# A windowed-attention and gated feed-forward kernel: queues ordered by a build-time list schedule, one load queue, f32 weight staging, filler matmuls

## The chip, the cores and the metric

One core of a Trainium2 chip runs the kernel. It has a matmul engine (TensorE, PE in the profile, with its weight loads shown as PEld), VectorE (DVE), ScalarE (ACT), GpSimd (POOL) and SyncE (SP), which issues DMAs. Each engine works through its own queue in order; semaphores order work between queues. The metric is the device time of one execution in microseconds, less is better.

## The reference

Four sequences of 768 tokens with 8 heads of 64 go through causal attention with a window of 128 keys and 4 "sink" keys that every query sees. The result, 3072 tokens of 512, goes through a feed-forward layer with a gated activation. All inputs and the output are f32.

```python
scores = scale * np.matmul(q, k.transpose(0, 1, 3, 2))
keep = is_sink | in_window            # pos < 4, or 0 <= query - key < 128
scores = np.where(keep, scores, -1e9)
a = softmax(scores)
x = np.matmul(a, v)                   # heads side by side: (3072, 512)
h = x @ w_in                          # (3072, 2048)
g = h * (1.0 / (1.0 + np.exp(-beta * h)))
out = g @ w_out                       # (3072, 512)
```

## The kernel before

The work is cut into 8 half-batches (hb) of 384 tokens; half-batch hb is half of sequence hb // 2. A half-batch of attention is 4 units u, each a pair of heads. The steps of the program, with their lines in the profile of before:

- **load** (L379) brings q, k and v in f32 into stage buffers, two of each. Half-batch 0 comes in small pieces (q and k by head pair, 192 KB each, v in three chunks of 256 KB), the others as whole q and k (768 KB) and three v chunks. **load_w** (L389) has GpSimd's DMA queue load the weights in 8 pieces of 1 MB and cast them to bf16 on the way.
- **cast** (L312 on DVE, L314 on ACT, L412 on POOL) makes bf16 copies: q and k to x16 (q_0, q_1, k_0, k_1 in the profile), v to vaug, which carries a column of ones.
- **T** (L432): 6 transposes of a unit on PE, then a copy to qkT. kS (L444) holds the sink keys, vS (L421) the sink values.
- **SC** (L485): the scores of a unit, 8 matmuls; exp on ACT into E (L495), two instructions; window masks on POOL (L501); a sink mask for the first half of a sequence (L509).
- **SS** (L519): scores against the sink keys, exp into ES (L522).
- **AV** (L547, L557): E and ES times v, with the sums from the column of ones; DVE takes the reciprocal (L561) and scales to onorm (L563).
- **OT** (L575): 3 transposes of onorm, then a copy to xT. When the four units of a half-batch are through, its 384 tokens are ready for the feed-forward part.
- **H** (HQ, L595): for a token block T_ (a half-batch) and one of 16 slices m of the hidden layer, 4 matmuls; tanh on ACT into t (L599), three buffers; the gate's product on DVE into g (L601). 64 H matmuls make a block.
- **O** (OQ, L613): 3 output tiles of a block, 16 matmuls each, in groups of 4; copy to osb, DMA out (L624).

A planner writes all queues while the program is built. It keeps an estimate of when each engine comes free (`G.free`) and asks in a loop which step's inputs and PSUM banks are ready; attention steps go before feed-forward steps, and H and O alternate. A step writes its matmuls and all that follows on the other engines at once, so each queue has the order in which steps were chosen. Where a copy can run on several engines, the one that would end first by the estimate is taken at that moment:

```python
def quickest(options):
    return min(options, key=lambda e: G.free[e] + options[e])
```

A cast of q, k or v is allowed on POOL only, but for half-batch 0, where DVE and ACT can take it. Loads are held back by bytes: `ordered` makes a load wait for the landing of an earlier one when more than `AHEAD_BYTES` = 3200000 lie between them, whichever queue that was on.

Of the kernel before, what the change touches and what calls it, by code (L numbers as in the profile page):

```python
# [22 lines left out]
class Op:  # L23
    __slots__ = ("eng", "fn", "deps", "signal", "count", "waits", "sem", "vc", "dma", "seq", "end")


class Graph:
# [3 lines left out]

    ENGINES = ("pe", "act", "dve", "gp", "sp")
    HOP = 180

    def __init__(self):
        self.ops = []
        self.writers = {}
        self.readers = {}
        self.last_x = {}
        self.n_dma = 0  # L40
        self.n_eng = {e: 0 for e in self.ENGINES}
        self.free = {e: 800.0 for e in self.ENGINES}
        self.dma_free = 0.0

    def add(self, eng, fn, ns=0, r=(), w=(), x=(), dma=None):

        o = Op()
        o.eng, o.fn, o.dma = eng, fn, dma
        o.signal, o.count, o.waits, o.vc = False, 0, [], None
        o.seq = self.n_eng[eng]  # L50
        self.n_eng[eng] += 1
        deps = []
        for k in r:
            ws = self.writers.get(k)
            assert ws, k
            deps += [(p, True) for p in ws.values()]
        for k in w:
            deps += [(p, False) for p in self.readers.get(k, {}).values()]
            deps += [(p, False) for p in self.writers.get(k, {}).values()]
        for k in x:  # L60
            deps += [(p, False) for p in self.last_x.get(k, {}).values()]
        o.deps = deps
        who = ("dma", self.n_dma) if dma else eng
        if dma:
            self.n_dma += 1
        for k in r:
            self.readers.setdefault(k, {})[who] = o
        for k in w:
            self.writers[k] = {who: o}
            self.readers[k] = {}  # L70
        for k in x:
            self.last_x.setdefault(k, {})[eng] = o
# [3 lines left out]
        if dma:  # L76
            self.free[eng] = at + (1150 if eng == "gp" else 550)
            self.dma_free = max(self.dma_free, at + 1100) + ns
            o.end = self.dma_free + 1000
        else:  # L80
            o.end = self.free[eng] = at + ns
        self.ops.append(o)
        return o

    def at(self, keys):

        t = 0.0
        for k in keys:
# [3 lines left out]
            t = max([t] + [p.end + self.HOP for p in ws.values()])  # L92
        return t

    def bank_at(self, k):
        return max([0.0] + [p.end + self.HOP for p in self.last_x.get(k, {}).values()])
# [83 lines left out]
def bass_streamingllm_window__then__act_swish_beta_kernel(  # L180
# [33 lines left out]
    _program(nc, G, sb, ps, q, k, v, moe_w_in, moe_w_out, moe_beta, out)  # L214
    G.resolve()
# [12 lines left out]
def _program(nc, G, sb, ps, q, k, v, w_in, w_out, beta, out):  # L228
    NU = 2 * NPAIR
    NSTG, NX, NV, NT, NE, NON, NG, NTT, NOS, NKS = 2, 2, 3, 8, 3, 3, 3, 3, 4, 4  # L230
# [24 lines left out]
    gt = sb("g", (128, NM, HALF), BF16, NG)  # L255
    tt = sb("t", (128, HALF), F32, NTT)
# [6 lines left out]
    AHEAD_BYTES = 3200000  # L263
# [22 lines left out]
    held = set()  # L286
# [18 lines left out]
    def quickest(options):  # L305

        return min(options, key=lambda e: G.free[e] + options[e])

    def copy_fn(eng, dst, src, scale=1.0):
        if eng == "dve":  # L310
# [3 lines left out]
        return lambda e: e.activation(dst, src, AF.Copy, bias=0.0, scale=scale)  # L314
# [29 lines left out]
    def beta_in():  # L344
        b_ = take(1)
# [6 lines left out]

    flight = []

    def ordered(nbytes):

        ahead, wait = 0, []
        for key, b_ in reversed(flight):
            ahead += b_
            if ahead > AHEAD_BYTES:  # L360
                wait = [key]
                break
        key = ("flight", len(flight))
        flight.append((key, nbytes))
        return wait, [key]

    def load(hb, n, i):
# [10 lines left out]
        wait, mine = ordered(dst.shape[0] * dst.shape[1] * dst.shape[2] * 4)  # L378
        add("act" if hb == 0 and n == "k" and i == 0 else "sp", lambda e: e.dma_start(dst, src), ns, r=wait,  # L379
# [418 lines left out]
```

## Time and profile before

| what | value |
|---|---|
| three runs | 249.97, 249.92 and 247.48 us, median 249.92 |
| profiled execution | 250.16 us |
| its span on the chip | 248.4 us |
| PE busy | 225.2 us, 91% |
| ACT, DVE, POOL busy | 164.4, 121.0 and 103.7 us |
| DMA | 29.69 MB counted, mean 120 GB/s; 27.27 MB read |

The profile shows one execution by instruction. A row of its timeline has the start and the length in us, the engine, the line of the kernel, the operation, output and inputs with shapes, and how many equal instructions the row merges; in brackets stand the engine's idle time ahead of it and what ended it. Matmuls overlap in the pipeline, so the length of one is more than the distance from one to the next.

### The profile page before, as it was taken

The page shows a single profiled execution, that of the slowest core. Times are in us where ns is not written, and L with a number is a line of the kernel's source. Part 1 is how long each engine was busy: PE and PEld are TensorE (multiplying, and loading weights), DVE is VectorE, ACT ScalarE, POOL GpSimd, SP SyncE. Part 2 cuts the span into 40 slices and gives each one's busy share as a digit, 9 for nine tenths or more (in the row PEclk, how much of TensorE's full clock was granted, in tenths as well). Part 3 has the DMA queues.
Part 4 walks back from the last instruction along what each step waited for, and adds up shares of the span by engine and source line. Part 5 has one row for each costly group of instructions (what it writes and reads, how often), then busy time and mean ns, then how long its engine had stood idle before and what let it go on. Part 6 is the DMA issues. An engine that isn't in the chain of part 4 may idle for free.

```text
span 248.4 us, 4941 instructions
## 1 busy us (share of the span) xinstructions
PE 225.2 (91%) x1862; PEld 131.7 (53%) x1889; DVE 121.0 (49%) x246; ACT 164.4 (66%) x296; POOL 103.7 (42%) x220
## 2 busy tenths in 40 slices
PE   2626898899998899999999999999999999999994
PEld 1415465565665567556575564655555555555531
DVE  2405375345567566467775465543533533453320
ACT  4754399827998688887976989754744644554420
POOL 7533391998773998718883423630000000000000
PEclk9999999999999999999999999999999999999999
DMA  6999899999999976700110101011111011111112
GB/s 199 219 215 296 180 181 249 239 256 264 303 244 267 314 189 210 163 3 4 45 45 0 45 0 45 0 45 42 42 42 45 1 44 45 42 42 42 45 44 84
DMA packets 49432, 29.69 MB, mean 120 GB/s; under 512 B 25840, under 2 KB 46336, under 8 KB 49408
## 3 DMA queue, kind: packets, MB, share of 16 engines
q1 hardware_dynamic: 44912, 24.98, 36.1%
q0 software_dynamic: 4224, 4.19, 10.5%
q8 instruction: 15, 0.25, 0.4%
q10 hardware_dynamic: 272, 0.20, 0.2%
q14 instruction: 9, 0.07, 0.1%
HBM read 27.27 MB, written 6.29 MB: 135 GB/s over the span
## 4 chain that ended last, share of the span: by engine, by line
PE 78%; ACT 7%; DMA 5%; DVE 3%; SPq 2%; issue 2%; POOL 1%; DVEq 0%
PE P L595 33%; PE P L613 30%; DMA v_stage<-in_v_dram 5%; PE P L557 4%; PE P L485 3%; ACT E L495 3%; PE P L432 3%; PE P L575 2%; SPq L379 2%; ACT qkT L314 1%; ACT t L599 1%; PE P L547 1%; DVE g L601 1%; DVE onorm L563 1%; PE P L519 1%
## 5 line engine op out<-in xcount | busy, mean ns | idle before, releaser
L601 DVE SCALAR_TENSOR_TENSOR g<-t,P 128x384 bf16<-128x384 f32 x128 | 69.8, 554 | 80.5 <-ACT t L599 67.0
L599 ACT ACTIVATE t<-P,hbeta 128x384 f32<-128x384 f32 x128 | 73.7, 588 | 43.7 <-PE P L595 39.3
L595 PE MATMUL P<-xT,w_in 128*128 128x384 bf16 x512 | 99.2, 332 | 0.6 <-DVE onorm L563 0.6
L613 PE MATMUL P<-w_out,g 128*128 128x512 bf16 x357 | 92.4, 379 | 2.7 <-ACT ES L522 0.7
L501 POOL TENSOR_SCALAR_AFFINE_SELECT E<-E 128x256 bf16<-128x256 bf16 (+1 forms) x112 | 52.3, 499 | 48.2 <-ACT E L495 47.8
L595 PEld LDWEIGHTS P<-xT,w_in 128*128 128x128 bf16 x512 | 49.5, 99 | 37.3 <-issue 2.2
L613 PEld LDWEIGHTS P<-w_out,g 128*128 128x128 bf16 x384 | 36.3, 98 | 35.6 <-DVE g L601 1.6
L495 ACT ACTIVATE E<-P 128x768 bf16<-128x768 f32 x64 | 45.2, 766 | 6.8 <-PE P L485 6.8
L557 PE MATMUL P<-vaug,E 128*128 128x65 bf16 x352 | 20.0, 199 | 6.7 <-DVE vaug L312 3.4
L557 PEld LDWEIGHTS P<-vaug,E 128*128 128x128 bf16 x352 | 17.5, 101 | 10.1 <-DVE vaug L312 3.6
L314 ACT ACTIVATE osb<-P 128x512 f32<-128x512 f32 x22 | 13.2, 598 | 13.5 <-PE P L613 13.2
L563 DVE TENSOR_TENSOR onorm<-P,rden 128x384 bf16<-128x384 f32 x32 | 17.8, 558 | 1.1
L314 ACT ACTIVATE qkT<-P 128x768 bf16<-128x768 bf16 x20 | 16.2, 828 | 1.4 <-PE P L432 1.4
L485 PE MATMUL P<-qkT 64*128 64x128 bf16 (+1 forms) x256 | 16.6, 251 | 0.1
L314 ACT ACTIVATE xT<-P 128x384 bf16<-128x384 bf16 x23 | 11.3, 497 | 6.8 <-PE P L575 6.7
L522 ACT ACTIVATE ES<-P 128x128 bf16<-128x128 f32 (+1 forms) x32 | 12.3, 402 | 3.9 <-PE P L519 3.7
L575 PE MATMUL P<-ident,onorm 128*128 128x128 bf16 x96 | 11.1, 230 | 2.5 <-DVE onorm L563 1.8
L412 POOL TENSOR_SCALAR_AFFINE_SELECT vaug<-v_stage 128x512 bf16<-128x512 f32 x21 | 13.3, 659 | 0.0
L485 PEld LDWEIGHTS P<-qkT 64*128 64x128 bf16 x256 | 8.9, 98 | 8.3 <-issue 3.6
L547 PE MATMUL P<-vS,ES 128*128 128x130 bf16 x64 | 13.0, 225 | 0.0
L312 DVE COPY qkT<-P 128x768 bf16<-128x768 bf16 x12 | 11.3, 952 | 1.8 <-PE P L432 1.6
L575 PEld LDWEIGHTS P<-ident,onorm 128*128 128x128 bf16 x96 | 7.4, 101 | 8.0 <-DVE onorm L563 2.5
(47 smaller groups left out, 124.5 us busy)
## 6 DMA issues: line engine op xcount, KB each, us to landing
v_stage<-in_v_dram SPq DMA_DIRECT2D x24, 256.0 KB, 6.2
out_dram<-osb SPq DMA_DIRECT2D x24, 256.0 KB, 2.0
q_stage<-in_q_dram SPq DMA_DIRECT2D x7, 768.0 KB, 6.2
k_stage<-in_k_dram SPq DMA_DIRECT2D x7, 768.0 KB, 8.3
w_in<-in_moe_w_in_dram POOLq DMA_DIRECT2D x4, 512.0 KB, 9.3
w_out<-in_moe_w_out_dram POOLq DMA_DIRECT2D x4, 512.0 KB, 7.3
q_stage<-in_q_dram SPq DMA_DIRECT2D x4, 192.0 KB, 3.7
k_stage<-in_k_dram SPq DMA_DIRECT2D x3, 192.0 KB, 4.3
```

The costliest lines, as they stand in the source:

```text
L314: return lambda e: e.activation(dst, src, AF.Copy, bias=0.0, scale=scale)
L485: add("pe", lambda e, dst=dst, kt=kt, kc=kc, rows=rows, q0=q0, nq=nq: e.matmul(dst, kt[rows, 1, kc:kc + 128], qkT[u % NT][rows, 0, q0:q0 + ...
L495: add("act", lambda e, src=src, dst_=dst_: e.activation(dst_, src, AF.Exp, bias=0.0, scale=SCALE), act_ns(256 * n), w=[(k_, z, j) for k_ i ...
L501: add("gp", lambda e, d=d, sg=sg, at_=at_: e.affine_select(d, d, [[0, 2 * len(at_)], [sg, 128]], ALU.is_ge, 0.0, base=min(sg, 0), channel_ ...
L547: add("pe", lambda e, m=m, c0=c0: e.matmul(A[:, c0:c0 + 2 * (D + 1)], ES[z][:, m * 128:(m + 1) * 128], vS[b % 2][:, 2 * hp:2 * hp + 2, :]. ...
L557: e.matmul(A[:, c0:c0 + D + 1], E[z][:, i, hh, :], vaug[vz][:, kb % NK, 2 * hp + hh, :], start=a, stop=o, skip_group_check=True), 39,
L563: add("dve", lambda e: e.tensor_tensor(onorm[on][:, :, :, :].rearrange("p m h d -> p (m h) d"), av[:, :, 0:D], rden[on][:, :].unsqueeze(2) ...
L575: add("pe", lambda e, m=m: nc.tensor.transpose(mp[:, m * 128:(m + 1) * 128], onorm[on][:, m, :, :].rearrange("p h d -> p (h d)"), ident[:, ...
L595: add("pe", lambda e, c=c: e.matmul(hp, w_in16[:, c, m * 128:(m + 1) * 128], xT[:, c, t0:t0 + HALF], start=(c == 0), stop=(c == 3)), mm_ns ...
L599: add("act", lambda e: e.activation(tt[ti][:, :], hp, AF.Tanh, bias=0.0, scale=hbeta[:, m:m + 1]), act_ns(HALF) + 93, r=["hbeta"], w=[("t" ...
L601: add("dve", lambda e: e.scalar_tensor_tensor(gt[T_ % NG][:, m, :], tt[ti][:, :], 1.0, hp, ALU.add, ALU.mult), dve_ns(HALF), r=[("t", ti)] ...
L613: add("pe", lambda e, m=m: e.matmul(P[:, bk, :], gt[T_ % NG][:, m, t * 128:(t + 1) * 128], w_out16[:, m, :], start=(m == 0), stop=(m == NM ...
```

## The change

The change keeps the steps and their arithmetic, and does six things.

1. **A list schedule.** The planner's loop still writes the program, but afterwards `Graph.arrange` orders every queue anew. PE's steps stay groups, of which the first three that are left can go next (`SKIP = 3`); an instruction of another engine can go as soon as its predecessors are planned; of those that can start first, the one with the longest tail behind it goes.
2. **Free engine choice.** A copy carries its alternatives (`alts`), and `arrange` takes the engine on which it would end first. Casts of q, k and v can now run on ACT, DVE or POOL; sink masks on POOL or DVE. The durations in these tables are new numbers.
3. **One load queue.** All loads are issued by SP, k's first piece too, which ACT issued before. `ordered` is gone. The order of loads is half-batches 0 and 1, then the weights.
4. **Weights in f32.** They come as 16 pieces of 512 KB by SP into six staging buffers (`wst`, three of them inside the g buffer of token block 2), and each is cast by ACT, DVE or POOL (`cast_w`). A piece's load waits for the cast of the piece six before it. H of block 2 is not written until all 16 are cast.
5. **The start is written out by hand**: the steps of half-batch 0 stand in a fixed order, with SC of unit 3 ahead of the AV steps. E has four buffers instead of three (`NE`).
6. **Filler matmuls**: 256-column matmuls of ones into PSUM bank 7, whose result nobody reads, stand where the plan has PE waiting, up to the last OT of half-batch 0. Bank 7 is held back for them until then.

```diff
+    def arrange(self):
...
+            for i, grp in enumerate(todo_pe[:self.SKIP]):
...
+                t, off = self.free["pe"], 0.0
+                for o in grp:
+                    t = max([t] + [p.end + self.HOP - off for p in o.preds if id(p) not in own and p.eng != "pe"])
+                    off += o.ns
+                if best is None or t < best[0] - self.SLACK:
+                    best = (t, "pe", i)
...
+            for o in pool:
+                opts = []
+                for e, (fn, ns) in o.alts.items():
+                    t = max(self.free[e], ready(o, e))
+                    if o.dma:
+                        t = max(t, self.dma_free - 3000)
+                    opts.append((t + ns, t, e))
+                _, t, e = min(opts)
+                by_eng.setdefault(e, []).append((t, o))
+            for e, c in by_eng.items():
+                t0 = min(c, key=lambda x: x[0])[0]
+                o = max((x for x in c if x[0] <= t0), key=lambda x: x[1].tail)[1]
+                if best is None or t0 < best[0]:
+                    best = (t0, e, o)
...
+                while self.filler and grp[0].group <= self.fill_to and self.free["pe"] + self.filler[0] <= t:
+                    o = self.filler[1]()
...
-    NSTG, NX, NV, NT, NE, NON, NG, NTT, NOS, NKS = 2, 2, 3, 8, 3, 3, 3, 3, 4, 4
+    NSTG, NX, NV, NT, NE, NON, NG, NTT, NOS, NKS, NWS = 2, 2, 3, 8, 4, 3, 3, 3, 4, 4, 6
...
+    wst = [w_[:, :, :] for w_ in sb("wst", (128, 2, 512), F32, NWS // 2)]
+    spare = gt[NG - 1][:, :, :].rearrange("p m t -> p (m t)").bitcast(F32).rearrange("p (z c f) -> p z c f", c=2, f=512)
+    wst += [spare[:, z, :, :] for z in range(NWS // 2)]
...
-    AHEAD_BYTES = 3200000
+    def any_of(alts, r=(), w=(), x=()):
+
+        return G.add(min(alts, key=lambda e: G.free[e] + alts[e][1]), None, 0, r, w, x, None, alts)
...
-    held = set()
+    held = {7}
...
-        add("act" if hb == 0 and n == "k" and i == 0 else "sp", lambda e: e.dma_start(dst, src), ns, r=wait,
-            w=[("stg", n, z, j) for j in keys] + mine, dma=f"d{n}{z}{'' if i is None else i}")
+        add("sp", lambda e: e.dma_start(dst, src), ns,
+            w=[("stg", n, z, j) for j in keys], dma=f"d{n}{z}{'' if i is None else i}")
...
-        add("gp", lambda e: e.dma_start(dst, src), 1048576 / 380, r=wait, w=[("w16", j)] + mine, dma=f"dw{j}")
+        add("sp", lambda e: e.dma_start(wst[j % NWS], src), 524288 / 370, w=[("wst", j % NWS)], dma=f"dw{j % NWS}")
+
+    def cast_w(j):
...
+        src_ = wst[j % NWS]
+        any_of(copies(dst, src_, {"act": 947, "dve": 602, "gp": 1060}), r=[("wst", j % NWS)], w=[("w16", m, h)])
...
+        if hb == 0 and n != "v":
+            ns = {"act": 413, "dve": 400}
         else:
-            fn = copy_fn(eng, dst, src)
-        add(eng, fn, opts[eng], r=r, w=w)
+            ns = {"act": 540, "dve": 340, "gp": 612}
+        any_of(copies(dst, src, ns), r=r, w=w)
...
-    LOADS = xl(0) + [0, 1, 2, 3] + xl(1) + [4, 5, 6, 7] + [x for hb in range(2, NSB) for x in xl(hb)]
+    LOADS = xl(0) + xl(1) + list(range(16)) + [x for hb in range(2, NSB) for x in xl(hb)]
...
+    G.fill(lambda e: e.matmul(P[:, 7, 0:256].rearrange("p (a b) -> p a b", a=2), ones[:, :],
+                              ones[:, :].unsqueeze(1).to_broadcast([128, 2, 128]), start=True, stop=True), ["ones"])
```

What this does to the queues is seen at three places. The first is SyncE's queue behind the small loads of half-batch 0; stage buffers ending in 1 belong to half-batch 1, and a name s_dw0 is the landing of weight piece 0. Before:

```order
L379 DMA v_stage0<-in_v_dram 128x8x64 x3
L379 DMA q_stage1<-in_q_dram 128x8x192 [waits s_dw0]
L379 DMA k_stage1<-in_k_dram 128x8x192 [waits s_dw1]
L379 DMA v_stage1<-in_v_dram 128x8x64 [waits s_dw2]
L379 DMA v_stage1<-in_v_dram 128x8x64 x2
L379 DMA q_stage0<-in_q_dram 128x8x192 [waits s_dw4]
```

And in the changed kernel, where wst and g2 are the weights' staging buffers:

```order
L491 DMA v_stage0<-in_v_dram 128x8x64 x3
L491 DMA q_stage1<-in_q_dram 128x8x192
L491 DMA k_stage1<-in_k_dram 128x8x192
L501 DMA wst0<-in_moe_w_in_dram 128x2x512
L501 DMA wst1<-in_moe_w_in_dram 128x2x512
L491 DMA v_stage1<-in_v_dram 128x8x64 x3
L501 DMA wst2<-in_moe_w_in_dram 128x2x512
L501 DMA g2<-in_moe_w_in_dram 128x2x512 x3
L501 DMA wst0<-in_moe_w_in_dram 128x2x512 [waits s_gp]
```

The loads of half-batch 1 no longer wait for weight landings; two weight pieces stand between its k and its v, and from the seventh piece on a load waits for a cast.

The second place is PE's queue from the last AV of half-batch 0 on. Before:

```order
L557 MATMUL P<-vaug,E 128x65 x6
L547 MATMUL P<-vS,ES 128x130
L557 MATMUL P<-vaug,E 128x65 x4
L575 MATMUL P<-ident,onorm 128x128 x3
L595 MATMUL P<-xT,w_in 128x384 x60
L432 MATMUL P<-ident,q_1 128x128 x3
```

In the changed kernel L671 and L661 are AV, L690 is OT, L885 the fillers, L548 T and L709 H:

```order
L690 MATMUL P<-ident,onorm 128x128 x3
L885 MATMUL P<-ones 128x256 x5
L690 MATMUL P<-ident,onorm 128x128 x3
L548 MATMUL P<-ident,q_1 128x128 x3
L548 MATMUL P<-ident,k_1 128x128 x3
...
L632 MATMUL P<-qkT,kS 128x384 x3
L600 MATMUL P<-qkT 128x2x128 x2
...
L709 MATMUL P<-xT,w_in 128x384 x8
L661 MATMUL P<-vS,ES 128x130
L671 MATMUL P<-vaug,E 128x65 x4
```

Half-batch 1's transposes and scores now stand ahead of the first H matmuls, and H comes in pieces between its AV steps; fillers stand only ahead of the last OT.

The third place is DVE's queue at half-batch 1 (L438 are casts and copies, L716 the product of H). Before, none of these casts was on DVE: behind onorm (L563) came 15 products (L601). Now:

```order
L438 CAST k_1<-k_stage 128x512
L438 COPY qkT<-P 128x768
L438 CAST w_in<-wst 128x2x512
L438 CAST vaug<-v_stage 128x8x64 x3
L675 RECIPROCAL rden<-P 128x6
L677 TENSOR_TENSOR onorm<-P,rden 128x384
L716 SCALAR_TENSOR_TENSOR g<-t,P 128x384 x2
L438 COPY xT<-P 128x384
L438 CAST w_in<-g 128x2x512
```

Casts of weights, of k and of v now stand in DVE's queue ahead of the products of H.

More of the change, by code (lines that the diff above doesn't have):

```diff
@@ L736, in _program @@
         now = G.free["pe"]
-        if not started and done["T"] >= 2:
-            beta_in()
-            started = True
         ffn = ("O", "H") if last == "H" else ("H", "O")
```

276 lines of the change are left out of this document (191 added, 85 removed).

## The prediction

> **What bounds the kernel now.** I read the profile from the coarse to the fine: its engine totals, a table of stages, then the timeline of TensorE around the first feed-forward matmul.
>
> ```profile
> PE 225.2 (91%) x1862; PEld 131.7 (53%) x1889; DVE 121.0 (49%) x246; ACT 164.4 (66%) x296; POOL 103.7 (42%) x220
> ...
> 0.00:26.00 26.00, 11.52 (x118) 8.10 (x119) 8.79 (x22) 13.46 (x25) 12.99 (x41) 1.00 1.04 232
> 26.00:54.40 28.40, 26.80 (x226) 15.43 (x227) 14.06 (x28) 19.56 (x33) 19.84 (x36) 1.00 1.00 215
> 54.40:172.90 118.50, 115.35 (x1151) 71.16 (x1166) 69.27 (x144) 95.73 (x177) 70.89 (x145) 1.00 0.45 121
> 172.90:248.40 75.50, 71.50 (x374) 36.99 (x379) 28.94 (x52) 35.66 (x61) 0.00 (x0) 1.00 0.11 43
> ```
>
> After the stage's length stand the busy times of PE, PEld, DVE, ACT and POOL, then granted clock, DMA share and GB/s. From 54.4 to 172.9 PE idles 118.50 - 115.35 = 3.15 us in all. The matmuls are the bound there, and there is little left to take. The first 26 us are another regime: PE is busy 11.52 of 26.00, while the DMA engines are full (share 1.04). So the start is limited by data. Its chain:
>
> ```profile
> 4.82 0.95 POOL L389 DMA_DIRECT2D w_in<-in_moe_w_in_dram  x1
> 4.84 4.10 SPq L379 DMA_DIRECT2D v_stage<-in_v_dram  x3
> ...
> 15.06 0.63 ACT L314 ACTIVATE vaug<-v_stage 128x512 bf16<-128x512 f32 x1 [1.37 <-DMA v_stage<-in_v_dram]
> 19.19 0.43 DVE L312 CAST vaug<-v_stage 128x512 bf16<-128x512 f32 x1 [5.01 <-DMA v_stage<-in_v_dram]
> 19.67 0.68 PE L557 MATMUL P<-vaug,E 128*128 128x65 bf16 x9 [3.42 <-DVE vaug L312]
> 25.51 0.50 PE L575 MATMUL P<-ident,onorm 128*128 128x128 bf16 x3 [0.88 <-DVE onorm L563]
> 25.81 12.34 PE L595 MATMUL P<-xT,w_in 128*128 128x384 bf16 x60
> ...
> 172.91 3.41 PE L595 MATMUL P<-xT,w_in 128*128 128x384 bf16 x20
> 176.16 1.03 PE L613 MATMUL P<-w_out,g 128*128 128x512 bf16 x4
> ```
>
> The third v chunk of half-batch 0, issued behind 4.84, lands only at 19.19, because the weight loads of GpSimd's queue share the DMA engines from 4.82 on. AV of unit 0 waits for it 3.42 us, OT of unit 3 runs at 25.51, and H starts at 25.81. Its first 60 matmuls take 12.34 us. At 172.91 twenty take 176.16 - 172.91 = 3.25 us, 0.1625 each, so 60 would be 9.75. The missing 2.6 us are matmuls at half rate, which the clock column does not show (1.00 everywhere); the durations do.
>
> **The change, part by part.** I compare both kernels at one milestone: half-batches 0 and 1 through OT and the 64 H matmuls of token block 0. Before, it lies behind OT of unit 7, and 32 O matmuls are done by then (groups of 4, 4, 4, 4, 8, 8; some records are missing):
>
> ```profile
> 42.00 0.81 PE L613 MATMUL P<-w_out,g 128*128 128x512 bf16 x3 [0.74 <-ACT ES L522]
> ...
> 52.52 1.89 PE L613 MATMUL P<-w_out,g 128*128 128x512 bf16 x7
> 54.25 0.33 PE L575 MATMUL P<-ident,onorm 128*128 128x128 bf16 x3
> 54.41 1.03 PE L613 MATMUL P<-w_out,g 128*128 128x512 bf16 x4
> ...
> 237.98 7.30 PE L613 MATMUL P<-w_out,g 128*128 128x512 bf16 x33 [0.26 <-DVE g L601]
> ```
>
> One O matmul is (7.30 - 0.38)/32 = 0.216 us (the last one's own 0.38 taken off), 32 are 6.9. Before, the milestone without O is therefore at 54.4 - 6.9 = 47.5 us. For the changed kernel I walk there:
>
> ```profile
> 8.15 1.30 ACT L495 ACTIVATE E<-P 128x768 bf16<-128x768 f32 x2 [0.65 <-PE P L485]
> 9.03 1.31 POOL L501 TENSOR_SCALAR_AFFINE_SELECT E<-E 128x256 bf16<-128x256 bf16 x3 [1.25 <-ACT E L495]
> 9.33 0.53 ACT L314 ACTIVATE q_0<-q_stage 128x384 bf16<-128x384 f32 x1
> 9.74 0.28 ACT L522 ACTIVATE ES<-P 128x128 bf16<-128x128 f32 x1
> ...
> 20.06 0.20 DVE L561 RECIPROCAL rden<-P 128x6 f32<-128x6 f32 x1
> 20.29 0.56 DVE L563 TENSOR_TENSOR onorm<-P,rden 128x384 bf16<-128x384 f32 x1
> ...
> q1 hardware_dynamic: 44912, 24.98, 36.1%
> q0 software_dynamic: 4224, 4.19, 10.5%
> ...
> 60.00:80.00 20.00, 19.21 (x197) 12.03 (x199) 11.74 (x26) 17.94 (x35) 13.02 (x25) 1.00 1.05 262
> ...
> q1 hardware_dynamic: 1439, 2.62, 10.0%
> ```
>
> *Half-batch 0.* No weights are in front any more: 2.36 MB of q, k and v from about 2 us on, at the 262 GB/s of the saturated stage 60 to 80, end at 11.0, so the last v chunk lands near 12. It is no longer last. What is last is ScalarE: four units of 1.30 + 0.28 and one cast of 0.53 are 6.85 us in one queue; from 8.6 (8.15, plus half a microsecond since k's first load now stands behind q's on SyncE) to 15.5. GpSimd's three selects of unit 3 end about 1 us later, 16.3; then AV 0.5, reciprocal and norm 0.76 and two handovers: OT of unit 3 at 17.9 instead of 25.5.
>
> *Half-batch 1.* A k cast stands on ScalarE behind the four xT copies, so the 24 transposes T start near 19.1. Three of the four qkT copies queue on ScalarE, 1.50/2 = 0.75 us each in the first row below: from the first unit's transposes at 19.5 to 22.0. SC of the second unit (0.44) and the first 8 H matmuls (1.3) follow, to 23.9.
>
> ```profile
> 38.66 1.50 ACT L314 ACTIVATE qkT<-P 128x768 bf16<-128x768 bf16 x2
> 40.23 0.50 PE L485 MATMUL P<-qkT 64*128 64x256 bf16 x8
> 40.67 0.59 PE L519 MATMUL P<-qkT,kS 128*128 128x384 bf16 x2
> 44.32 0.22 PE L547 MATMUL P<-vS,ES 128*128 128x130 bf16 x1
> 44.85 0.33 PE L519 MATMUL P<-qkT,kS 128*128 128x384 bf16 x1
> ...
> L412 POOL TENSOR_SCALAR_AFFINE_SELECT q_1<-q_stage 128x512 bf16<-128x512 f32 x12 | 7.5, 659 | 0.0
> L312 DVE CAST vaug<-v_stage 128x512 bf16<-128x512 f32 x1 | 0.4, 429 | 5.0 <-DMA v_stage<-in_v_dram 5.0
> ```
>
> The first AV of this half-batch also needs v1, behind 5.77 MB of one queue: 2 + 22.0 + 1 = 25.0 at 262 GB/s, somewhat earlier since 1 MB of it is weights. I take 24.5. From there the work in the written order is AV 4 x 0.53 (44.85 - 44.32), SC 2 x 0.44 (40.67 - 40.23), OT 4 x 0.16 (54.41 - 54.25) and 56 H matmuls, 9.1: 12.8 us. One weight piece is cast on GpSimd between two units' selects; a 1024-element cast has no row, twice the 0.66 above is its upper end and once the lower; with the selects ahead of it I add 1.2. Milestone: 38.5. That is 24.5 + 12.8 + 1.2. Against 47.5 the **gain is 9.0 us**.
>
> *Weights.* The 16 pieces of 512 KB are the unknown, as no f32 weight load stands in the trace. The nearest row is 2 KB packets out of SBUF (170 to 240 us): 2.62 MB in 10.0% of 70 us, 374 GB/s, 1.40 us a piece. The old weight queue read 8.39 MB in 10.5% of 248.4 us: 1.63 a piece. The slow end is the mixed 262 GB/s, 2.0 a piece. I take 1.5, near the first two: the last piece, 14 behind v1, lands at about 45 and is cast by DVE at 45.7. O of block 0 wants it at 38.5 + three O groups 2.6 + 32 H matmuls 5.2 = 46.3. Just hidden. At 2.0 it is 24.5 + 28 + 0.7 = 53.2, and of the 9.0 us only 2.1 are left. Each load waits for the cast six pieces earlier; six times 1.5 leaves 9 us for a slot to be landed, cast and issued again. Behind a waiting weight load SyncE holds all loads of half-batch 2: at 1.5 its q and k land 6 us after the last weight, 51, and its T stands 12.8 us of matmuls behind the milestone, at 51.3. So this too is just hidden, and slips by what the weights slip.
>
> *Fillers.* 47 matmuls of 256 columns, about 0.11 us each at full rate by the O matmul, 0.22 at half. All stand before OT of unit 3, where ScalarE's chain is late, not PE; cost nothing. Without that cover they would cost 5 to 10 us. If they keep PE at full rate, the 2.6 us of slow H are gone; this is inside the walk, which uses full-rate prices from 19 us on. Bank 7, held for them, leaves seven; SC takes four. The fourth E buffer lets SC of unit 3 go ahead of AV, which is in the walk.
>
> *Casts moved.* GpSimd loses 44 of its 63 casts at 0.66 (29 us), and DVE takes most, at 0.43, and seven more qkT copies. DVE's 58% of the stage 54 to 173 (69.27 of 118.50) becomes about 75%, ScalarE stays at 81%. Both stay below PE. The wider choice and the lookahead over three groups can save up to the 3.15 us of PE idle; a queue order fixed from planned times can as well add as much. I take no change, and keep -3 and +3.
>
> *The end.* From 172.9 on the order is H and O alone in both. No change.
>
> **Sum.** The profiled execution took 250.16 us, 1.7 beyond its span of 248.4. 250.16 - 9.0 = 241.2; the median of the runs is 0.24 lower than the profiled one, so **241.0**.
>
> **Rivals.**
>
> *Weights pace PE* (0.14). The mixed rate holds, or a cast stands late in its queue and holds its slot: up to 250.16 - 2.1 - 0.24 = 247.8. For it: before, SyncE also stood idle for handovers, below. Against: the 374 GB/s.
>
> ```profile
> SPq L379 <- DMA w_in<-in_moe_w_in_dram: 13.0, 3, 5.6
> SPq L379 <- DMA w_out<-in_moe_w_out_dram: 12.1, 3, 7.1
> SPq L379 <- POOL vaug L412: 9.4, 3, 6.5
> ...
> v_stage<-in_v_dram SPq DMA_DIRECT2D x24, 256.0 KB, 6.2
> ```
>
> *The slow rate comes back* (0.14). Between OT of unit 3 and AV of unit 4 PE has pauses and no fillers; before, a PE busy less than half of 26 us ran at half rate, and needed 5 us of unbroken H to leave it (2.6 us lost at half rate). Then T, SC and H until 24.5 take up to 4 us more, of which the wait for v1 hides most, and another 4.6 us at half rate cost 2.3: together about 3.6, 244.6. Against: PE idled 1.6 us of 26.0 to 54.4 (28.40 - 26.80), in pieces, and H kept its 0.16 spacing at 172.91. [...]
>
> *Slower: casts that wait in DVE's queue* (0.09). The order is fixed, and DVE now holds most q, k and v casts between the g products of H. One cast whose load is late stops every g behind it; three t buffers cover about 2 us, then PE stops. v chunks land 6.2 us (median, the row above) after their issue, so a late issue costs up to 4.2. In each of half-batches 2 to 7 an average of 1.5 us decides: 6 x 1.5 = 9.0. At 2.1 it is 253.6. Against: a half-batch is loaded in 9 us and used in about 20, and SyncE runs ahead.
>
> *It doesn't do what it says* (0.07): the planned start is not reached, since the planner's durations are shorter than the measured ones (413 ns for the k cast that took 0.53 us), and the lists hold each other up: 249.9.
>
> **How the numbers follow.** Forecast 0.50 (239 to 243.5); a middle stage without its idle time, 238, 0.06; the rivals as above. The range goes from 236.5, the forecast with idle and a start 1.5 us better, to 248.5, the slow weights: it leaves out the slower case and a part of the last. About 1% is what a measurement of this kernel can tell from no change, so faster means below 247.4: the forecast, the better middle stage, the clock case and most of the weights case, 0.80; same 0.11; slower 0.09.
>
> **What would show it.** First H matmul near 22 us with 0.16 us spacing; OT of unit 3 near 18; the last v chunk of half-batch 0 cast by 14; OT of unit 7 near 38.5; the last weight cast by 46; PE idle of about 3 us from there to the last attention unit. The prediction is wrong if H is spaced 0.32 us, if PE waits for weight casts beyond 40 us, or if g waits for DVE's casts in the middle.

## The result, and the profile after

| kernel | median of its runs (range) | profiled execution | span |
|---|---|---|---|
| before | 248.70 us (246.9 to 249.97, 4 runs) | 250.16 us | 248.4 us |
| after | 240.71 us (240.04 to 240.98, 4 runs) | 240.98 us | 239.3 us |

The ratio is 0.968, with a 95% interval of 0.9601 to 0.9759. Measured again later beside other kernels, after took 240.43 us (6 runs). The forecast was 241.0. The total came out as forecast, but the terms of the sum did not: the start won 2.8 us less than forecast, and 2.9 us came from two stretches that the sum had put at nothing.

The engine totals of after, then its table of stages in the columns used above: the start up to 26 us, to the milestone (OT of unit 7), to the last attention unit, and the rest. After's figures stand in the order span, PE, PEld, DVE, ACT, POOL, clock, DMA share, GB/s.

```profile
PE 228.4 (95%) x1936; PEld 132.3 (55%) x1936; DVE 149.4 (62%) x305; ACT 163.7 (68%) x293; POOL 79.6 (33%) x172
...
q1 hardware_dynamic: 49536, 33.57, 48.6%
```

```profile
0.00:26.00 26.00, 20.93 (x235) 13.68 (x236) 16.42 (x35) 17.58 (x33) 16.97 (x47) 1.00 0.96 252
26.00:42.10 16.10, 13.84 (x133) 8.17 (x130) 13.78 (x30) 13.23 (x24) 7.78 (x14) 1.00 1.03 374
42.10:160.00 117.90, 117.51 (x1169) 70.94 (x1168) 88.65 (x186) 94.27 (x171) 54.88 (x113) 1.00 0.57 151
160.00:239.30 79.30, 76.12 (x410) 39.49 (x405) 30.59 (x56) 38.63 (x67) 0.00 (x0) 1.00 0.12 44
```

In the middle PE now idles 117.90 - 117.51 = 0.39 us, where it idled 3.15 before. From 26.0 to 42.1 it still idles 16.10 - 13.84 = 2.26 us, and DVE is the fullest engine beside it, 13.78 of 16.10. All traffic but instructions runs in one queue, and the weights come at 374 GB/s. PE's busy time rose by 3.2 us although the slow H are gone, since the fillers are in it (47 records, 8.8 us together).

The timeline of after around the milestone, PE and then DVE and ACT:

```profile
18.08 0.34 PE L690 MATMUL P<-ident,onorm 128*128 128x128 bf16 x3 [0.63 <-DVE onorm L677]
...
23.92 1.47 PE L709 MATMUL P<-xT,w_in 128*128 128x384 bf16 x8
25.23 0.22 PE L661 MATMUL P<-vS,ES 128*128 128x130 bf16 x1
...
30.04 2.45 PE L709 MATMUL P<-xT,w_in 128*128 128x384 bf16 x14 [0.80 <-DVE w_in L438]
...
33.70 1.80 PE L709 MATMUL P<-xT,w_in 128*128 128x384 bf16 x10 [0.19 <-DVE w_in L438]
...
41.96 0.34 PE L690 MATMUL P<-ident,onorm 128*128 128x128 bf16 x3 [1.10 <-DVE onorm L677]
```

```profile
13.20 0.62 DVE L438 CAST vaug<-v_stage 128x512 bf16<-128x512 f32 x1
...
24.21 0.70 DVE L438 CAST vaug<-v_stage 128x512 bf16<-128x512 f32 x1 [0.43 <-DMA v_stage<-in_v_dram]
...
29.11 0.87 DVE L438 CAST w_in<-g 128x1024 bf16<-128x1024 f32 x1 [0.90 <-DMA g<-in_moe_w_in_dram]
...
40.68 0.19 DVE L675 RECIPROCAL rden<-P 128x6 f32<-128x6 f32 x1
40.79 0.65 DVE L438 CAST w_out<-g 128x1024 bf16<-128x1024 f32 x1
41.35 0.55 DVE L677 TENSOR_TENSOR onorm<-P,rden 128x384 bf16<-128x384 f32 x1
...
46.55 1.05 ACT L433 ACTIVATE w_out<-wst 128x1024 bf16<-128x1024 f32 x1
```

The third v chunk of half-batch 0 is cast at 13.20 instead of 19.19, OT of unit 3 stands at 18.08 instead of 25.51, the first H at 23.92. Eight H take 1.31 us (23.92 to 25.23), 0.164 each, full rate. Then PE waits twice for casts of w_in; ahead of the first of these, at 29.11, DVE itself stands idle 0.90 us until the piece of w_in has landed. The last OT waits for onorm, which stands in DVE's queue behind a cast of w_out. At the end, nothing waits between the last H and the last 36 O matmuls:

```profile
226.89 1.46 PE L709 MATMUL P<-xT,w_in 128*128 128x384 bf16 x8
228.19 7.93 PE L729 MATMUL P<-w_out,g 128*128 128x512 bf16 x36
```

Before had two pauses there, one ahead of the row at 237.98 and one ahead of this:

```profile
237.33 0.39 PE L613 MATMUL P<-w_out,g 128*128 128x512 bf16 x1 [0.25 <-DVE g L601]
```

To compare kernels whose matmuls stand in different orders I keep a **ledger**: the time at which a step starts on PE, less the time that all matmuls ahead of it in PE's queue need at their full-rate distance (H 0.1625 us, O 0.216, attention's by their rows, fillers nothing). What is left, an estimate, is what PE lost until then. Differences between columns give the loss of a stage.

| profiled execution | OT of unit 3 at | lost there | lost at OT of unit 7 | lost at OT of unit 31 | lost at PE's end |
|---|---|---|---|---|---|
| before | 25.51 | 20.03 | 24.79 | 29.25 | 30.17 |
| after | 18.08 | 12.60 | 18.54 | 20.95 | 21.01 |
| after, again | 17.98 | 12.50 | 17.51 | 19.81 | 19.87 |

So 24.79 - 18.54 = 6.25 us were won up to OT of unit 7, 4.46 - 2.41 = 2.05 in the middle and 0.92 - 0.06 = 0.86 in the last stretch; together 9.16, the fall of PE's end from 245.28 to 236.12. The start of one and the same kernel scatters by about 1 us between executions.

### The profile page after: what moved, and what is told of

Read it like the earlier page. It is cut to its first block, busy times and chain, and to the rows that moved or that the text cites. A ratio compares the mean times of both kernels' runs of the same rounds, so it can differ in the third digit from the quotient of the medians.

```text
span 239.3 us, 4895 instructions
## 1 busy us (share of the span) xinstructions
PE 228.4 (95%) x1936; PEld 132.3 (55%) x1936; DVE 149.4 (62%) x305; ACT 163.7 (68%) x293; POOL 79.6 (33%) x172
## 4 chain that ended last, share of the span: by engine, by line
PE 80%; SPq 9%; DVE 4%; DMA 3%; ACT 2%; issue 1%
PE P L729 34%; PE P L709 31%; SPq L491 7%; PE P L600 4%; PE P L548 4%; PE P L671 3%; DMA g<-in_moe_w_in_dram 3%; PE P L690 2%; SPq L501 2%; DVE g L716 1%; PE P L632 1%; PE P L661 1%; ACT t L714 1%; ACT E L609 1%; DVE w_in L438 1%
## 5 line engine op out<-in xcount | busy, mean ns | idle before, releaser
L716 DVE SCALAR_TENSOR_TENSOR g<-t,P 128x384 bf16<-128x384 f32 x128 | 69.9, 552 | 59.2 <-ACT t L714 56.6
L709 PE MATMUL P<-xT,w_in 128*128 128x384 bf16 x512 | 98.5, 326 | 1.1 <-DVE w_in L438 1.0
L729 PE MATMUL P<-w_out,g 128*128 128x512 bf16 x384 | 97.3, 379 | 0.0
L615 POOL TENSOR_SCALAR_AFFINE_SELECT E<-E 128x512 bf16<-128x512 bf16 (+1 forms) x112 | 54.5, 516 | 56.1 <-ACT E L609 55.3
L709 PEld LDWEIGHTS P<-xT,w_in 128*128 128x128 bf16 x512 | 48.0, 98 | 37.5 <-DVE w_in L438 1.8
L609 ACT ACTIVATE E<-P 128x768 bf16<-128x768 f32 x64 | 45.7, 769 | 3.1 <-PE P L600 2.8
L438 DVE COPY qkT<-P 128x768 bf16<-128x768 bf16 x19 | 18.0, 951 | 4.0 <-PE P L548 4.0
L671 PE MATMUL P<-vaug,E 128*128 128x65 bf16 x352 | 18.8, 193 | 0.8 <-DVE vaug L438 0.7
L433 ACT ACTIVATE osb<-P 128x512 f32<-128x512 f32 x21 | 12.5, 597 | 10.2 <-PE P L729 10.1
L671 PEld LDWEIGHTS P<-vaug,E 128*128 128x128 bf16 x352 | 16.7, 97 | 3.4 <-DVE vaug L438 0.9
L433 ACT ACTIVATE xT<-P 128x384 bf16<-128x384 bf16 x20 | 9.9, 495 | 6.7 <-PE P L690 6.7
L600 PEld LDWEIGHTS P<-qkT 64*128 64x128 bf16 x256 | 8.6, 94 | 10.6 <-issue 5.1
L433 ACT ACTIVATE qkT<-P 128x768 bf16<-128x768 bf16 x13 | 10.2, 814 | 5.2 <-PE P L548 5.1
L690 PE MATMUL P<-ident,onorm 128*128 128x128 bf16 x96 | 10.7, 220 | 2.3 <-DVE onorm L677 2.2
L661 PE MATMUL P<-vS,ES 128*128 128x130 bf16 x64 | 12.7, 220 | 0.0
L690 PEld LDWEIGHTS P<-ident,onorm 128*128 128x128 bf16 x96 | 7.0, 98 | 7.7 <-DVE onorm L677 4.2
L885 PE MATMUL P<-ones 128*128 128x256 bf16 x47 | 8.8, 323 | 1.1 <-POOL ones L444 1.1
```

What stands on the lines that cost most here:

```text
L438: return lambda e: e.tensor_copy(dst, src)
L600: add("pe", lambda e, dst=dst, kt=kt, kc=kc, rows=rows, q0=q0, nq=nq: e.matmul(dst, kt[rows, 1, kc:kc + 128], qkT[u % NT][rows, 0, q0:q0 + ...
L609: add("act", lambda e, src=src, dst_=dst_: e.activation(dst_, src, AF.Exp, bias=0.0, scale=SCALE), act_ns(256 * n), w=[(k_, z, j) for k_ i ...
L615: add("gp", lambda e, d=d, sg=sg, at_=at_: e.affine_select(d, d, [[0, 2 * len(at_)], [sg, 128]], ALU.is_ge, 0.0, base=min(sg, 0), channel_ ...
L671: e.matmul(A[:, c0:c0 + D + 1], E[z][:, i, hh, :], vaug[vz][:, kb % NK, 2 * hp + hh, :], start=a, stop=o, skip_group_check=True), 39,
L690: add("pe", lambda e, m=m: nc.tensor.transpose(mp[:, m * 128:(m + 1) * 128], onorm[on][:, m, :, :].rearrange("p h d -> p (h d)"), ident[:, ...
```

## The experiments

**Theory A:** the start was won by the order of loads and of the lists together; the middle and the end by the lookahead over three PE groups. Rivals: the fillers' clock, the spread of casts over engines, the f32 staging.

### Fillers, arrangement, lookahead, casts: after with one part taken away

`nofill`: no filler matmuls.

```diff
-    G.fill(lambda e: e.matmul(P[:, 7, 0:256].rearrange(...), ones[:, :], ...
```

> The changed kernel without its 47 filler matmuls, nothing else. Theory A (the fillers keep the matmuls at full rate from 6 us on): without them PE is busy too little until the first unbroken H, so transposes, scores and H between 19 and about 30 us run at half rate; 56 matmuls of H and half-batch 1 then cost 2.5 to 4 us more: 243.5 to 245, H spaced 0.32 us at first. Rival (the start is paced by loads and casts, PE's rate is hidden in the waits): 240.5 to 241.5 even with H spaced 0.32 us.

Measured: 240.60 us (240.09 to 240.97), ratio 0.9671 [0.9605, 0.9737]; the same as after. Theory A's price for the fillers falls. The matmuls do run slower without them. Three transposes of half-batch 0, first in after, then here:

```profile
9.63 0.33 PE L548 MATMUL P<-ident,q_0 128*128 128x128 bf16 x3
```

```profile
9.64 0.50 PE L548 MATMUL P<-ident,q 128*128 128x128 bf16 x3
```

The clock column reads 1.00 in both, as it does in the first 26 us of before. At 16.70 three take 0.33 us here too, and then the granted clock falls. Stages of this kernel around T of half-batch 1, columns as above:

```profile
16.80:20.00 3.20, 1.54 (x23) 1.06 (x20) 1.78 (x5) 1.75 (x4) 1.63 (x2) 1.00 1.13 335
20.20:23.40 3.20, 3.20 (x24) 1.63 (x23) 2.15 (x4) 3.17 (x6) 0.53 (x1) 0.50 0.84 166
23.60:27.00 3.40, 3.19 (x41) 1.93 (x38) 1.82 (x5) 3.40 (x8) 3.06 (x6) 1.00 0.97 295
```

Between 20.2 and 23.4 the granted clock is 0.50 and PE is busy without a gap with transposes and scores, while ScalarE is busy 3.17 of 3.20 with the copies and exponentials that these feed. In after PE does the same work at full clock and waits 0.15, 0.37 and 0.36 us for ScalarE in between. The first H comes at 23.95 here and at 23.92 there, and in both the first eight take 1.31 us, full rate. The half rate is hidden behind ScalarE.

`noarrange`: no list order and no fillers; the queues stay as the planner's loop wrote them.

```diff
-    G.arrange()
-    G.fill(...)
```

> The changed kernel with the queues left in the order in which the planner's loop wrote them, and so without fillers, which only the list schedule places. Everything else stays: one load queue, f32 weights, free choice for each copy at the moment it is written. Theory A (the list schedule is what took out the 3 us of PE idle in the middle): 3 us over the run without fillers, PE idle of 3 us or more after 54 us. Rival (spread casts and the fourth E buffer took it out): within 1 us of the run without fillers.

Measured: 245.39 us (244.43 to 245.82), ratio 0.986 [0.979, 0.993]. Against nofill the list order is worth 4.8 us. In the ledger 21.81 are lost at OT of unit 7 against nofill's 17.67, that is 4.1 in the start; the rest falls on the middle (3.0 against 2.4) and on the wait for g at the end (0.85 against 0.07), which is back here. Theory A put 3 us into the middle; the list order is worth 0.6 there. Even without it and its lookahead the middle loses 1.5 us less than the 4.46 of before. How much of the 4.1 is the clock no run separates: it is granted at 0.50 here from 14.8 to 25.0 (mean 0.80 over the first 26 us).

`skip1`: the list order may not look past the next PE group.

```diff
-    SKIP = 3
+    SKIP = 1
```

> The list schedule without lookahead on PE: only the next group of matmuls can go. Theory A (PE passes a group that waits): idle of PE after 42 us grows from 0.4 to 2 to 3 us and the wait ahead of the last O groups comes back, 0.7: 243 to 244. Rival (the order of the other engines' queues does it): within 1 us of 240.7.

Measured: 243.14 us (242.28 to 244.26), ratio 0.9777 [0.9701, 0.9854], 2.4 us behind after. The start is untouched (17.28 lost at OT of unit 7). The middle loses 4.10, nearly the 4.46 of before, and at the end the pauses of before are back:

```profile
227.31 1.46 PE L709 MATMUL P<-xT,w_in 128*128 128x384 bf16 x8
228.82 0.38 PE L729 MATMUL P<-w_out,g 128*128 128x512 bf16 x1
229.38 0.39 PE L729 MATMUL P<-w_out,g 128*128 128x512 bf16 x1 [0.18 <-DVE g L716]
230.03 7.29 PE L729 MATMUL P<-w_out,g 128*128 128x512 bf16 x33 [0.26 <-DVE g L716]
```

The last O group needs the g of the last H. With a lookahead of three, PE takes O groups first whose g is long there; with one, it stands. That the middle needs the lookahead holds for this list order; noarrange has neither and loses less there.

`poolcasts`: q, k and v of half-batches 1 to 7 are cast on GpSimd alone, as before.

```diff
-            ns = {"act": 540, "dve": 340, "gp": 612}
+            ns = {"gp": 612} if hb else {"act": 540, "dve": 340, "gp": 612}
```

> The q, k and v casts of half-batches 1 to 7 on GpSimd only, as before; all the rest as in the changed kernel. Theory A (spreading the casts removed the idle of the middle): 2 to 3 us of PE idle come back after 54 us, and the six casts of half-batch 1 at 0.66 in one queue put T some 2 us later: 243 to 245. Rival (the casts on DVE are a cost: DVE's queue held onorm back 1.1 us at 41 us): the middle stays without idle and the start loses only the 2 us of T, 241 to 242.5.

Measured: 239.80 us (239.49 to 240.84), ratio 0.9637 [0.9559, 0.9714]. Both theories miss (243 to 245, and 241 to 242.5). It is not slower than after: the spread of these casts is not what filled the middle. The interval overlaps after's, so that it is faster isn't shown. With all its fillers in place, its granted clock still fell to 0.50 between 20.1 and 23.3.

### Load order and choice of engine: before with one part of the change

`b_loads`, and once more as `b_loads_again`: half-batch 1 is loaded ahead of all weights.

```diff
-    LOADS = xl(0) + [0, 1, 2, 3] + xl(1) + [4, 5, 6, 7] + ...
+    LOADS = xl(0) + xl(1) + [0, 1, 2, 3, 4, 5, 6, 7] + ...
```

> The kernel before with one edit: the loads of half-batch 1 stand ahead of all weights in the load list, as in the kernel after. Weights are still cast by the transfer on GpSimd's queue, and the order of every other queue is written by hand as before. Theory A (the start's gain comes from two things, the load order and the list order): OT of unit 3 comes near 20 to 22 us instead of 25.5, the ledger at OT of unit 7 falls by 2 to 4 us of the 24.8 before, nothing changes later, about 246 to 248. Rival B (only the list order gives the gain, because the weights just come late instead): 249 to 251.

> The kernel before with one edit once more: the loads of half-batch 1 stand ahead of all weights, nothing else. In the profile taken first, the ledger at OT of unit 7 had lost 21.8 us against 24.8 before. Theory A (load order alone is worth these 3 us): 245.5 to 247 where before has 248.8. Rival B (the late weights take it back later): 248.5 to 250.

Measured: 254.66 us (246.62 to 255.55, 4 runs; no interval), and again 253.27 us (250.62 to 254.29, 6 runs) with a ratio of 1.0152 [1.0083, 1.0222]. Both theories miss: the load order alone makes the kernel **slower** in nine of ten executions. It does win the start: OT of unit 3 at 20.97 and 20.73, and 21.77 and 20.60 lost at OT of unit 7 against 24.79. Between OT of units 11 and 15 it loses 10.8 and 9.3 us, where before loses 1.0. The timeline of the second profile there, DVE, POOL and PE, then its stages:

```profile
71.98 5.22 DVE L421 COPY vS<-vaug 4x260 bf16<-4x260 bf16 x2 [4.14 <-POOL vaug L412]
77.23 1.49 DVE L601 SCALAR_TENSOR_TENSOR g<-t,P 128x384 bf16<-128x384 f32 x3
...
71.28 1.28 POOL L412 TENSOR_SCALAR_AFFINE_SELECT vaug<-v_stage 128x512 bf16<-128x512 f32 x2
72.50 1.95 POOL L501 TENSOR_SCALAR_AFFINE_SELECT E<-E 128x256 bf16<-128x256 bf16 x4
74.39 0.67 POOL L412 TENSOR_SCALAR_AFFINE_SELECT vaug<-v_stage 128x512 bf16<-128x512 f32 x1
75.00 1.89 POOL L412 TENSOR_SCALAR_AFFINE_SELECT q<-q_stage 128x512 bf16<-128x512 f32 x3
...
77.84 0.50 PE L432 MATMUL P<-ident,q 128*128 128x128 bf16 x3 [5.18 <-DVE g L601]
```

```profile
72.70:76.50 3.80, 0.00 (x0) 0.00 (x0) 3.80 (x1) 0.00 (x0) 3.80 (x8) 1.00 1.09 362
76.70:83.30 6.60, 5.22 (x33) 3.23 (x33) 4.38 (x12) 3.61 (x7) 2.42 (x6) 0.50 0.98 227
```

A small copy of sink values stands in DVE's queue ahead of the g products. It waits 4.14 us for a v cast on POOL, a time in which PE still has work, and then itself takes 4.99 us, until POOL's unbroken row ends (below); in that time PE stands 5.18 us. After this pause the clock is granted at half (0.50 from 76.7 to 83.3), in the first profile for 10.2 us. Pause and half rate together are most of the 9.3 and 10.8 us. It is akin to the slower rival of the prediction, since one instruction in DVE's queue stops every g behind it, but no load was late: POOL works without a pause from 63.5 to 76.9.

In the first profile of b_loads, too, PE waits 5.2 us for a g, once. In before the longest such copy took 0.655 us; in after, after again, nofill, poolcasts, pcast_nofill and wsw all eight together took 2.0 to 3.0. The one run of ten that took 246.62 us, as theory A expected, was not profiled; its mean granted clock was 0.997, in the three others of its group 0.973 to 0.986, so it hardly had this half rate. Where the pause stays away, the load order alone may well be worth the 2 us of theory A. after has the same order of half-batch 1 and weights and no such pause, but neither has noarrange, whose queues stand as the loop wrote them: that the list order is what removes it isn't shown.

`b_choice`: in before, casts of all half-batches may go to any engine.

```diff
-        if hb == 0:
-            opts["dve"] = dve_ns(size)
-            opts["act"] = act_ns(size) + 90
+        opts["dve"] = dve_ns(size)
+        opts["act"] = act_ns(size) + 90
```

> The kernel before with one edit: the copies of q, k and v of every half-batch may go to VectorE, ScalarE or GpSimd by the planner's costs, instead of only those of half-batch 0; order and loads stay. Theory A (what removed TensorE's 3 us of idle time in the middle and the last wait for g is the lookahead of the list order): within 1% of before, 248.5 to 251. Rival C (free choice of engine removed it): 2 to 3 us faster, 246.5 to 247.5.

Measured: 249.80 us (248.14 to 252.42, 10 runs) beside before's 248.76, ratio 1.0042 [0.9995, 1.0088]: no difference, as theory A has it. The start loses 22.66 in this execution, 2.1 less than before, but the middle 5.54, 1.1 more.

### Could the start be won whole? After with other loads and casts

`wfirst`: w_in ahead of half-batch 1, w_out behind it.

```diff
-    LOADS = xl(0) + xl(1) + list(range(16)) + ...
+    LOADS = xl(0) + list(range(8)) + xl(1) + list(range(8, 16)) + ...
```

> The kernel after with one edit: the eight pieces of w_in stand ahead of the loads of half-batch 1 in the load list, the eight pieces of w_out behind them. Theory A (after OT of unit 3 TensorE lost time because the first attention group of half-batch 1 came while w_in was still being cast, and the casts of w_in, w_out, q, k and v crowded on VectorE from 20 to 42 us): with w_in early, H of half-batch 0 fills TensorE from OT of unit 3 on while half-batch 1 loads, and the ledger's loss at OT of unit 7 falls from 18.5 to 13 to 15 us; about 236 to 238. Rival D (VectorE's queue is full anyway, so the same casts only come in another order): 240 to 242. Rival E (half-batch 1 now comes late and TensorE waits for it behind H, as with the weights' first pieces in the kernel before): 242 to 246.

Measured: 246.38 us (245.63 to 248.06, 10 runs), ratio 0.9911 [0.9877, 0.9945]. Rival E's mechanism holds, at the upper end of its 242 to 246, and theory A falls; 23.75 are lost at OT of unit 7. PE's timeline:

```profile
18.54 8.78 PE L709 MATMUL P<-xT,w_in 128*128 128x384 bf16 x50
27.61 2.45 PE L709 MATMUL P<-xT,w_in 128*128 128x384 bf16 x14 [0.29 <-DVE w_in L438]
...
32.74 0.80 PE L548 MATMUL P<-ident,k 128*128 128x128 bf16 x3 [2.51 <-DVE k L438]
```

H runs unbroken from 18.54 to 30 us, as hoped; then PE has nothing but half-batch 1, which comes late, and no H is left to fill the gaps of its attention. In this kernel H is worth more between the attention units than ahead of them.

`wsw`: weights written as bf16 by the transfer itself, on GpSimd's queue, in the load order of after.

```diff
-        add("sp", lambda e: e.dma_start(wst[j % NWS], src), ...
+        add("gp", lambda e: e.dma_start(dst, src), ..., w=[("wsw", j), ("w16", m, h)], dma=f"dw{j}")
```

> The kernel after with one edit: the weights are not staged in f32 and cast by an engine; each of the 16 pieces is written as bf16 straight into its place by the transfer, issued on GpSimd's queue, with the load order unchanged. Theory A (the casts of the weights on VectorE cost the start what TensorE waited for w_in and for onorm behind w_out, 0.8 + 0.2 + 1.1 us): about 238.5 to 239.5. Rival F (a casting transfer is slower, as the 2.0 us per 512 KB before showed, so H waits for the weights instead): 241 to 246.

Measured: 250.75 us (249.67 to 253.94, 10 runs), ratio 1.0102 [1.0052, 1.0152]; rival F's mechanism, well beyond its 241 to 246. The casting transfers took 10.6% of 16 engines' 247.6 us for 8.39 MB of weights, 1.64 us for 512 KB, against 1.40 at after's 374 GB/s; before had 1.63, and rival F's 2.0 is the rate of its q, k and v loads, 262 GB/s. The second queue takes the DMA engines from the v loads again (third v chunk cast at 17.50, in after at 13.20; OT of unit 3 at 21.33), and H waits for the weights:

```profile
37.51 1.80 PE L711 MATMUL P<-xT,w_in 128*128 128x384 bf16 x10 [0.91 <-DMA w_in<-in_moe_w_in_dram]
...
43.02 0.48 PE L711 MATMUL P<-xT,w_in 128*128 128x384 bf16 x2 [1.99 <-DMA w_in<-in_moe_w_in_dram]
...
44.73 2.45 PE L711 MATMUL P<-xT,w_in 128*128 128x384 bf16 x14 [1.22 <-DMA w_in<-in_moe_w_in_dram]
```

26.73 are lost at OT of unit 7, 8.2 more than in after. The staging, with the single queue, is what the load order rests on.

`wnodve`: the weights are cast on ScalarE and GpSimd only.

```diff
-        any_of(copies(dst, src_, {"act": 947, "dve": 602, "gp": 1060}), ...
+        any_of(copies(dst, src_, {"act": 947, "gp": 1060}), ...
```

> The kernel after with one edit: the 16 casts of the weights may go to ScalarE or GpSimd, no longer to VectorE, which had 11 of them. Theory A (the start lost 0.8 + 0.2 us to casts of w_in and 1.1 us to onorm behind the casts of w_out in VectorE's queue): the ledger's loss at OT of unit 7 falls from 18.5 to 16.5 to 17.5 us; about 239 to 239.8. Rival G (the 1.05 us casts of the other two engines make H wait as long, or hold exp or the masks back): loss at OT of unit 7 of 18.5 to 20 us; 240.5 to 242.

Measured: 242.52 us (241.87 to 243.35, 6 runs) beside 240.43 for after, 2.1 us slower; theory A falls, rival G is nearest (240.5 to 242). The waits for w_in and for the last onorm are gone from PE's rows. That DVE was their cause doesn't follow, since the list came out in another order: the first H stands at 28.96, where after has it at 23.92. And the clock fell back over AV and H this time:

```profile
27.20:30.40 3.20, 2.83 (x23) 1.75 (x24) 0.76 (x2) 3.20 (x6) 2.75 (x6) 0.50 1.01 351
```

```profile
28.96 2.24 PE L709 MATMUL P<-xT,w_in 128*128 128x384 bf16 x8
31.03 0.33 PE L690 MATMUL P<-ident,onorm 128*128 128x128 bf16 x3
```

Eight H take 31.03 - 28.96 = 2.07 us instead of 1.31. The milestone itself can't be read here, since this list has only 40 H ahead of OT of unit 7; by OT of unit 11 20.24 are lost against 19.27 in after (18.24 in its second profile).

`pcast_nofill` and `after_again`: the two best single edits together, beside after.

> The kernel after with two edits: q, k and v of half-batches 1 to 7 are cast on GpSimd only, and the filler matmuls are left out. If both single edits add up (0.9 us faster and nothing), 239.5 to 240; if the casts on GpSimd were worth nothing beyond the scatter of the runs, 240.4 to 241.

> The kernel after itself, beside the others on the same chip, to compare versions that differ by less than 1%: 240.0 to 241.0.

Measured: 240.66 us (239.95 to 241.39) and 240.43 us (239.85 to 241.27), 6 runs each. The gain of poolcasts doesn't come back; no version tried is shown to beat after. In the profile of pcast_nofill three transposes still take 0.53 us at 21.40, and the first H comes at 24.76: half rate up to there, and the same time. Over the whole profile its transposes of q and k average 243 and 241 ns, in after 220 to 225.

## Why the prediction was right, and where it was not

- **Bound and cause of the start: right.** Loads, not matmuls, bound the first 26 us of before (DMA share 1.04, PE busy 11.52 of 26.00). With the weights behind, the v chunk is cast at 13.20 (by 14), OT of unit 3 stands at 18.08 (17.9), T at 18.25 (19.1). The first H comes at 23.92 at full rate, 1.5 us later than the walk's 22.4 (22.0 and SC of the second unit): T and SC wait for k casts (0.49 and 0.21) and for ScalarE (0.15, 0.37 and 0.36). b_loads shows that the load order alone moves OT of unit 3 from 25.51 to 20.7 to 21.0.
- **Milestone at 38.5, gain 9.0: the mis-sized term.** The H behind OT of unit 7 begins at 42.14; less 4 O matmuls that is 41.3, so the gain was 47.5 - 41.3 = 6.2 us. Of the 2.8 missing, 0.7 is the first AV of half-batch 1 (25.23, not 24.5), which stands behind the late H; v1 no longer holds it. From there the walk had 12.8 of work and 1.2 of waits, 14.0; measured are 41.3 - 25.2 = 16.1. Four waits stand in rows, 0.17 + 0.80 + 0.19 + 1.10 = 2.26. A bracket begins only when the last matmul has ended; from start to start, less the full-rate distance, the same four are 0.35 + 0.96 + 0.36 + 1.27 = 2.9, 1.7 more than allowed; the last 0.4 is made of gaps too short for a row. I had let GpSimd be late with one weight cast. The 0.17 is ScalarE's exp. The 1.10 and the 0.19 are DVE's queue, where weight casts, g and onorm share 13.78 of 16.10 us. The 0.80 is a piece of w_in that landed late, as DVE's idle time at 29.11 shows; the walk asked when O needs its weights and never when H does. In the second execution of after that cast began at 27.99 without waiting for a landing, PE waited 0.2 us for w_in in all, and 1.0 us less was lost (17.51), so a part of the miss is scatter.
- **Weights at 1.5 us a piece: right.** 374 GB/s in the stage 26 to 42.1 is 1.4 a piece; the last cast begins at 46.55 (the walk had 45.7), and no O waits for it. The rival that weights pace PE is there in small, in the 0.80 above.
- **Fillers cost nothing: right; that they hold the rate: true in after, and worthless.** That fillers keep PE at full rate was my assumption behind the walk's full-rate prices from 19 us on, and no run shows that it holds in general. In after three transposes take 0.50 us at 4.87 and 0.33 from 8.13 on. nofill has the half rate in its first 16 us and again for 3.4 us, and the same time (240.60); its H run at full rate all the same, eight in 1.31 us, so the 2.6 us of slow H are gone without the fillers too. poolcasts, with them, fell back for 3.4 us and is no slower (239.80). The clock rival (0.14, 244.6) named a thing that happens, in the place it named, when the fillers are away; its price was wrong there, since ScalarE was late anyway (3.17 of 3.20 us busy). Where the fall-back met AV and H (wnodve, eight H in 2.07 us) or followed a long wait (b_loads, 5.18 us), matmuls that PE needed ran slower. The fall-back lasted 3.4 us in nofill, and 10.2 and 6.8 in the two profiles of b_loads. In nofill it came after a stretch, 16.8 to 20.0, in which PE was busy 1.54 of 3.20 us, nearly all of it transposes, with no pause over 0.96. In poolcasts PE was busy 1.67 of 3.40 us ahead of it (16.6 to 20.0), with five fillers beside the transposes, and in wnodve it came after AV, scores and one OT, with a pause of 0.67 us and no H. What sets it off, and what ends it, no run shows.
- **Middle: no change; measured, 2.05 us won.** My step was that the wider choice and the lookahead may save up to 3.15 us or cost as much, and I put it at nothing. It saved. By what is only in part shown: skip1 loses 4.10 there, so the list order needs its lookahead, but noarrange, with neither, loses 3.0, so about 1.5 of the 2.05 came with the other parts. Free choice alone did not bring it (b_choice loses 5.54), nor did the spread of casts (poolcasts loses 1.85). DVE stood at 88.65 of 117.90, 75%, as forecast, and PE idled 0.39 us in all.
- **End: no change; measured, 0.86 us won.** I looked at the order of H and O, and not at the 0.9 us in which the last O group waits for the last g (rows 237.33 and 237.98 of before, the second of which I had quoted for O's price). skip1 and noarrange have them again, so the lookahead removes them.
- **The sum** was right by luck: 9.0 + 0 and 6.2 + 2.9 are both about 9.

The parts can't be priced apart: load order alone loses 1.5%, free choice alone does nothing, the list order without staging (wsw) loses 1%, everything but the list order and the fillers (noarrange) wins 1.4%. Together they win 3.2%. The start written by hand and the fourth E buffer stand in noarrange and in every version of after; no run takes them out, so what they are worth stays open.

## What to carry to other kernels

A better order of loads can uncover a pause elsewhere that costs more than the start gains (b_loads lost 10.8 and 9.3 us for 3.0 and 4.2 gained): in the new profile, look for small instructions ahead of what PE needs that wait (4.14 us there) or take many times their usual length (4.99 us, in before 0.22 to 0.655). Matmuls whose data is there are filler; keep them between steps with pauses rather than running them off at once (wfirst did, and took 246.38 us). Before paying for a clock, look which engine is late in the stretch where it is low (ScalarE in nofill, 3.17 of 3.20 us busy).

## What was not expected of the hardware

- A 4x260 copy on VectorE lasted 4.99 us. By line, of b_loads' second profile and of before (shortest, median and longest in ns, then first and last start):

```profile
L421 DVE COPY vS<-vaug x2: 221/2606/4991, 72.0 to 77.0; 4x260 bf16<-4x260 bf16 x2
```

```profile
L421 DVE COPY vS<-vaug x8: 220/597/655, 13.7 to 116.8; 4x260 bf16<-4x260 bf16 x8
```

  In before three of the eight, beside which POOL ran no cast (at 13.7, 14.0 and 55.7), took 0.22 us; the five that began during one of POOL's casts of 0.66 took 0.60 to 0.655 and ended within 0.1 us of that cast. The one of 4.99 us begins at 71.98, 0.1 us after the second cast of POOL's row of casts and masks, and ends at 76.97, just after that row's last (75.00 + 1.89 = 76.89). So it ended only after nine instructions of POOL (that cast and the eight from 72.50 on), while the copy of 0.655 us at 55.07 in before ended at 55.73, just after one cast (54.38 + 1.27 = 55.65 for the row). What made it so long, and why it spans one instruction in before and nine here, is open; no run varied it.
- The granted clock fell to 0.50 for 3.4 us in the profiles of nofill, poolcasts, wfirst and wnodve, for 10.2 in that of noarrange, and for 10.2 and 6.8 in the two of b_loads.
- A 1024-element cast from f32 in after took 0.69 us on VectorE (median of 11; 0.65 at 40.79) and 1.05 on ScalarE (46.55) and GpSimd, less than twice the 0.43, 0.62 and 0.66 that its v casts of 512 elements took there (medians).
